# Attention of two entries ahead of the FFN, with the last keys' scores of two head pairs on quarters of the array

## The chip, the cores and the metric

One Trainium2 chip, one core of it. The metric is the device time of one execution in microseconds (us), lower is better. Three runs of the kernel before gave 1162.48, 1165.79 and 1167.2 us; the median is 1165.79.

## The reference

Three blocks follow each other, for 4 batch entries of 448 positions, in fp32 throughout:

```python
# attention: 12 heads of 64, scores capped by tanh
scores = cap * tanh(q @ k.T / sqrt(64) / cap)
attn = softmax(scores)
x = attn @ v                       # heads joined: 4 x 448 x 768
# FFN with LayerNorm and residual, d_ff = 3072
x = x + relu(layernorm(x) * g_ln @ w_ch1) @ w_ch2
# gMLP
h = relu(x @ w_in); u, v = halves of h (512 each)
v_s = w_spatial @ normalize(v) + b_spatial[:, None]
out = (u * v_s) @ w_out
```

## The kernel before

Everything is held transposed: channels on the 128 partitions, the 448 positions along the free axis. Two heads make a pair that fills 128 partitions (64 channels each), so an entry has 6 pairs and the program 24.

**Attention of a pair** (`emit_load`, `emit_s`, `emit_st`, `emit_v`, `emit_n`). The 448 keys are three chunks of 128 and a tail of 64, the "last keys". Scores come out with keys on the partitions. `emit_s` makes the scores of chunks with two fp32 matmuls each (64 x 128 weights, the two heads on the two row halves of the array) into one double PSUM bank ("two"; there are 2); `expo` applies tanh and exp on ScalarE (ACT), the second in place in SBUF ("es"). `emit_st` makes the last keys' scores of both heads in one full-array matmul: the weights hold the last 64 keys of the two heads as diagonal blocks (extra 128 columns of the tile "qk", loaded by two small DMAs, zero elsewhere). `emit_v` adds the exponentials of the chunks on VectorE (DVE), multiplies them with v (128 x 64 weights, the two heads on the two column halves) and with ones (the softmax sums). The last keys' part of v is a full-array matmul with diagonal blocks; the last keys' part of the sums is another one with the constant `blocks` in the first 16 heads, and is folded into the DVE sum (`fold`) in later ones. Sums are inverted by `invert`, by way of DRAM: two rows out, repacked onto 128 partitions, reciprocal, back, broadcast; `FAST` lists the pair that takes the reciprocal directly instead. `emit_n` multiplies, and adds to LayerNorm's sum over channels.

An fp32 matmul shows as two instructions in the trace. "bank" is one of 4 single PSUM banks, "hs" a 128 x 448 SBUF tile, "vt" the tile of v.

**FFN and gMLP** use fp32r with each operand split into a high and a low part, three matmuls per product. Weights come from DRAM in their raw 64-bit form; `weight` rebuilds them (ACT, DVE), keeps a copy in DRAM ("kept") for the next use, and splits them (`wh` slots). `h_unit` is one 128-channel block of the hidden layer for one entry (18 matmuls), `y_unit` one block of the output (12 matmuls); NG = 6 groups of 4 hidden blocks. `ln_mean` and `ln_scale` make LayerNorm; the latter has matmuls of two columns and a round trip by DRAM.

**Order of the work.** `main` writes the program order. Before: the pairs of entry 0 and two pairs of entry 1 (`LEAD = 4` heads) run without FFN beside them (the lead), with 5 weight blocks of w1 prepared early (`EARLY`). Then 2 groups (`SOLO`) of entry 0 run alone, with entry 1's other four pairs between them, then the same 2 groups of entry 1, then the other 4 groups for both entries, which share each weight block. The 12 pairs of entries 2 and 3 are spread between these units. The gMLP of entries 0 and 1 follows, then FFN and gMLP of entries 2 and 3.

`attend` gives each step of a pair its place, in units of one pair's share. `Program` records all operations, gives each a due time from `Recorder`'s cost estimates, and `plan` writes each engine's final order by list scheduling: an engine takes the ready operation that is due first, not more than 28 us ahead (`AHEAD`), if its buffers fit. `prog.either` lets the planner choose between two engines; `prog.group` keeps matmuls together. All DMAs are issued on one queue, SP.

Of the kernel before, what the change touches and what calls it, by code (L numbers as in the profile page):

```python
# [34 lines left out]

SOLO = 2, 0
LEAD = 4
FILL = 0.45

AHEAD_HEADS = 12  # L40

LOAD = 1.05


FAST = (), (11,)

COUNTS = 16, 8, 11, 3, 2, 2, 3, 6, 2, 1

# [7 lines left out]

EARLY = 5

# [362 lines left out]
class Recorder:  # L421
# [3 lines left out]
    def __getattr__(self, method):  # L425
# [5 lines left out]
        def record(*args, **kw):  # L431
# [5 lines left out]
            if self.name == "PE":  # L437
                rows = min(kw["rhs"].ap[0][1], kw["out"].ap[0][1])
                cost = 4 * n / 2400 + 0.004 if kw["rhs"].dtype == F32 else n / 2400 + 0.0133
                if rows <= 64:  # L440
                    cost *= 0.55
            elif self.name == "D":
                cost, latency = 0.5, 4 * out.size() / 360e3
            elif self.name == "A":
                cost = (0.13 if psum_in else 0.16) + n / 1200
                cost += 0.094 if hasattr(kw.get("scale"), "tensor") else 0.0
            elif self.name == "P":
                cost = 1.0 if "pow" in repr(args) + repr(kw) else 0.45 + n / 500
            elif method == "reciprocal":
                cost = 0.15 + n / 160  # L450
            elif method in ("tensor_copy", "tensor_scalar") and not psum_in:
                cost = 0.14 + n / 1920
            else:
                cost = 0.14 + n / 960
# [12 lines left out]
def attn_ffn_gmlp_kernel(  # L467
# [35 lines left out]
    def slots(name, n, shape, dt, pool=const):  # L503
# [4 lines left out]
            ("rs", [128, 2, S], F32R), ("rb", [128, 2, DH], F32R), ("hs", [128, S], F32),  # L508
            ("rc", [128, 2 * S // 128], F32), ("w6", [128, DM, 2], I32), ("wr", [128, DM], F32),
            ("wh", [128, 2, DM], F32R), ("es", [128, 2, S], F32), ("qk", [128, 2 * S + 128], F32),  # L510
            ("small", [128, 80], F32)), COUNTS))

    vts = slots("vt", 2, [128, 4, 128], F32)
# [3 lines left out]
    blocks = const.tile([128, 128], F32, name="blocks")  # L517
    ones32 = const.tile([128, 2], F32, name="ones32")
# [93 lines left out]
    xsp = {}  # L612
    sums = {}

    def emit_load(i):
# [16 lines left out]
        raws[i] = t, u  # L632

# [5 lines left out]
    def emit_s(i, cs):  # L639

        t, u = raws[i]
        scs = [twos.get()[:, :, 0:S] for _ in cs]
# [24 lines left out]
    def invert(name, rows, outs):  # L667

        n = len(rows)
        d0 = dram.tile([n, S], F32, name=f"sum_{name}")  # L670
        d1 = dram.tile([n, S], F32, name=f"inv_{name}")
        c = rcs.get()
# [11 lines left out]

    def emit_v(i):


        b, h = heads[i]
        E = st.pop(i)
        u, et = st.pop(("t", i))  # L690
        s = es.get()
        add(s, E[0], E[1])
        add(s, s, E[2])
        fold = i >= H + LEAD
        if fold:
            for half in range(2):
                r = slice(64 * half, 64 * half + 64)
                add(s[r, half], s[r, half], et[r])
        ps, pr = banks.get()[:, 0:S], banks.get()[:, 0:S]
        with prog.group(0.4):  # L700
            T.matmul(out=ps, lhsT=u[:, 3], rhs=et, start=True, stop=False)
            if not fold:
                T.matmul(out=pr, lhsT=blocks, rhs=et, start=True, stop=False)
            for o, e, w in [(ps, e, u[:, c]) for c, e in enumerate(E)] + [(pr, s, None)]:
                for half in range(2):
                    r = slice(64 * half, 64 * half + 64)
                    T.matmul(out=o[r], lhsT=ones64 if w is None else w[:, r], rhs=e[:, half],
                             start=fold and w is None, stop=e is E[-1] or w is None)
        x, R = xts[b][h // 2] if b < 2 else hs.get(), hs.get()
        cp(x, ps, (A, V))  # L710
        if b < 2 and h + 1 in FAST[b]:
            V.reciprocal(R, pr)
        else:
            cp(R, pr, (A, V))
            invert(f"{b}_{h}", [R[0:1], R[64:65]], [R[0:64], R[64:128]])
        sums[i] = x, R

# [148 lines left out]
    def sp_unit(b, i, sp, bias):  # L866
# [10 lines left out]
        mm3(ps, terms)  # L877
        w, x = hs.get(), hs.get()
        V.tensor_tensor(w, ps, bias, ALU.add)
        with prog.either():  # L880
            for e in (V, P):
                e.tensor_tensor(x, w, us[b][i], ALU.mult)
        if b % 2:
# [85 lines left out]

    def attend(first, n, per, start=0.0, ahead=True):  # L970
        todo = []
        for j in range(0, n, 2):
            i = first + j
            t = start + per * j
# [3 lines left out]
            todo += [(t + x * per, fn, a) for x, fn, *a in stages if ahead or a[0] < first + n]  # L978
        return todo

    def norm(b, t):
        return [(t, ln_mean, (b,))]

    def main():
        emit_load(0)
        SP.dma_start(out=capt, in_=cap)
        SP.dma_start(out=g_t, in_=g_ln)
        P.memset(ones64, 1.0)
        P.memset(blocks, 0.0)
        for half in range(2):  # L990
            r = slice(64 * half, 64 * half + 64)
            P.memset(blocks[r, r], 1.0)
        P.memset(ones32, 1.0)
# [7 lines left out]
        group = FG * 3 * KD + KD * 3 * FG  # L1001
        more = H + LEAD
        for p in range(NP):
            one, two = bs = (2 * p, 2 * p + 1)
            solo = SOLO[p]
            end = H * (two + 1)

            def alone(b):
                return chain(*(x for g in range(solo) for x in (h_units((b,), g, 2), y_units((b,), g, False))))


            n = end - more
            total = solo * group
            per = max(total, 1) * FILL / max(n, 1)
            if p:
                drive(alone(one), attend(more, n, per) + ([(per * (n + 2.3), ln_load, (two,))] + norm(two, per * (n + 2.3) + 1e-6) if n else []))
            else:
                drive(alone(one), attend(more, n, per) + norm(two, per * (n + 2.3)))
            more = end
# [5 lines left out]
            drive(units, attend(more, n, total / max(n, 1), ahead=False))  # L1025
            more += n
            nxt = [] if p + 1 == NP else [two + 1] if AHEAD_HEADS < H else [two + 1, two + 2]
            gmlp(bs, nxt)
            emit_load(more)

    main()
    with tc.manual_schedule():
        t = tok_t[0][0]
        nc.vector.memset(t[:], 0.0)
        nc.scalar.activation(out=t[:], in_=t[:], func=ACTF.Tanh)
        for t in vts.tiles:
            nc.gpsimd.memset(t[:], 0.0)
        for t in qks.tiles:
            nc.gpsimd.memset(t[:, 2 * S:2 * S + 128], 0.0)
        prog.issue()  # L1040
# [54 lines left out]
```

## Time and profile before

| what | value |
|---|---|
| median of three runs | 1165.79 us |
| the profiled execution, device time | 1166.69 us |
| its span, first to last instruction | 1164.9 us |
| TensorE (PE) busy | 1131.2 us, 97% of the span |
| weight loads (PEld) | 916.9 us, 79% |
| VectorE (DVE) | 715.0 us, 61% |
| ScalarE (ACT) | 430.2 us, 37% |
| mean granted TensorE clock | 0.993 |

The profile is one execution, traced by the hardware. Busy time is the union of an engine's instructions. Matmuls are pipelined and their ends are modelled, so the distance from one start to the next tells more than an instruction's own duration, and a TensorE that is always busy need not be at its peak. A wait names what ended it: the engine and the tile that it released. The granted clock is a share of TensorE's full speed.

### The profile page before, as it was taken

To read this page: it belongs to the slowest core of one execution; us is meant where nothing else is said; L and a number is where in the kernel's file an instruction comes from. 1 tells how busy PE (TensorE), PEld (TensorE's weight loads), DVE (VectorE), ACT (ScalarE), POOL (GpSimd) and SP (SyncE) were. 2 spreads that over 40 slices of the span, in tenths; PEclk is the share of its full clock that TensorE was granted. 3 is DMA by queue.
4 is the path that set the end of the run, shared out by engine and by line. 5 is a ranking of instruction groups with operands and counts; after the bars stand their busy time and mean duration, and the time that the engine had idled before them with its cause. 6 is when DMAs were issued, how large, how long until landed. Compare 5 with 4: busy or idle time off the path is not lost.

```text
span 1164.9 us, 14179 instructions
## 1 busy us (share of the span) xinstructions
PE 1131.2 (97%) x5300; PEld 916.9 (79%) x5300; DVE 715.0 (61%) x1188; ACT 430.2 (37%) x638; POOL 22.2 (2%) x30
## 2 busy tenths in 40 slices
PE   7979989999999999999989989999999999999998
PEld 2326667878887777787769779999999999998878
DVE  5548788767576666766979883534343434384751
ACT  6978636344344444344433451011111111120311
POOL 0000000000000000000000100000000000000010
PEclk9999999999999999999999999899999999999999
DMA  7545556556355545655366422212121212124302
GB/s 217 154 116 160 148 158 192 142 172 185 115 165 156 158 134 167 196 158 150 124 187 210 165 70 66 64 52 63 47 69 41 68 41 68 42 71 118 111 17 104
DMA packets 88577, 140.97 MB, mean 121 GB/s; under 512 B 41486, under 2 KB 53692, under 8 KB 88508
## 3 DMA queue, kind: packets, MB, share of 16 engines
q1 hardware_dynamic: 88508, 140.06, 40.7%
q8 instruction: 42, 0.69, 0.2%
q14 instruction: 27, 0.22, 0.1%
HBM read 107.99 MB, written 32.03 MB: 120 GB/s over the span
## 4 chain that ended last, share of the span: by engine, by line
PE 86%; DMA 7%; DVE 4%; SPq 2%; ACT 1%; issue 1%; ACTq 0%; DVEq 0%
PE bank L459 80%; PE two L459 5%; DMA w<-in_w_u_dram 2%; SPq L459 2%; DVE wr L459 1%; DMA hs<-inv 1%; DMA rc<-sum 1%; DMA wr<-kept_w 1%; DVE wh L459 1%; DMA qk<-in_qk_dram 1%; DMA inv<-rc 1%; DVE hs L459 0%; DVE x L459 0%; ACT es L459 0%; DMA w<-in_w_dram 0%
## 5 line engine op out<-in xcount | busy, mean ns | idle before, releaser
L459 PE MATMUL bank<-rs,wh 128*128 128x448 f32 x2070 | 428.5, 366 | 5.1 <-ACT es L459 4.1
L459 PEld LDWEIGHTS bank<-rs,wh 128*128 128x128 f32 x2070 | 389.9, 189 | 41.2 <-ACT es L459 4.6
L459 PE MATMUL bank<-rb,wh 128*128 128x448 f32 x1872 | 391.6, 368 | 7.2 <-ACT wh L459 2.1
L459 PEld LDWEIGHTS bank<-rb,wh 128*128 128x128 f32 x1872 | 353.6, 190 | 43.6 <-issue 5.4
L459 ACT ACTIVATE wh<-wr 128x512 fp32r<-128x512 f32 (+1 forms) x101 | 72.1, 714 | 236.5 <-PE bank L459 201.1
L459 DVE TENSOR_TENSOR x<-bank,x 128x448 f32<-128x448 f32 x144 | 89.6, 623 | 100.9 <-PE bank L459 99.8
L459 ACT ACTIVATE rb<-bank 128x448 fp32r<-128x448 f32 x96 | 52.4, 546 | 239.2 <-PE bank L459 239.2
L459 DVE TENSOR_TENSOR wh<-wr,wh 128x512 fp32r<-128x512 f32 (+1 forms) x167 | 130.2, 781 | 9.5 <-ACT wh L459 4.9
L459 DVE SCALAR_TENSOR_TENSOR rb<-bank,rb 128x448 fp32r<-128x448 f32 x96 | 59.9, 624 | 111.7 <-ACT rb L459 111.4
L459 DVE SCALAR_TENSOR_TENSOR wr<-w,wr 128x512 int32<-128x512 int32 (+1 forms) x152 | 120.4, 792 | 2.5
L459 ACT ACTIVATE wr<-w 128x512 f32<-128x512 f32 (+1 forms) x76 | 57.4, 756 | 81.4 <-DVE wh L459 24.8
L459 ACT ACTIVATE es<-two,qsc 128x896 f32<-128x896 f32 x72 | 70.3, 1004 | 26.6 <-PE two L459 26.6
L459 PE MATMUL two<-qk 64*128 64x448 f32 x288 | 71.8, 591 | 8.5 <-ACT es L459 4.2
L459 ACT ACTIVATE es<-es,capt 128x896 f32<-128x896 f32 x72 | 72.5, 1040 | 0.0
L459 DVE CAST wh<-wr 128x512 fp32r<-128x512 f32 (+1 forms) x66 | 30.7, 466 | 65.7 <-PE bank L459 45.6
L459 DVE TENSOR_TENSOR es<-es,es 128x896 f32<-128x896 f32 x48 | 52.1, 1086 | 23.3 <-ACT es L459 23.0
L459 PE MATMUL bank<-es,vt 128*64 128x448 f32 x288 | 59.4, 548 | 0.0
L459 PEld LDWEIGHTS two<-qk 64*128 64x128 f32 x288 | 25.4, 192 | 40.8 <-issue 21.2
L459 ACT ACTIVATE hs<-bank 128x448 f32<-128x448 f32 x54 | 29.4, 545 | 72.9 <-PE bank L459 69.7
L459 DVE TENSOR_SCALAR wr<-wr 128x512 int32<-128x512 int32 (+1 forms) x76 | 35.8, 472 | 26.4 <-ACT wr L459 26.4
L459 PEld LDWEIGHTS bank<-es,vt 128*64 128x64 f32 x288 | 18.5, 136 | 37.9 <-issue 34.2
L459 PE MATMUL bank<-rs,rb 128*128 128x448 f32 (+1 forms) x192 | 43.7, 381 | 0.0
(86 smaller groups left out, 666.8 us busy)
## 6 DMA issues: line engine op xcount, KB each, us to landing
w<-in_w_dram SPq DMA_DIRECT2D x24, 768.0 KB
w<-in_w_dram SPq DMA_DIRECT2D x36, 512.0 KB
wr<-kept_w SPq DMA_DIRECT2D x32, 384.0 KB
wr<-kept_w SPq DMA_DIRECT2D x48, 256.0 KB
qk<-in_qk_dram SPq DMA_DIRECT2D x48, 224.0 KB
kept_w<-wr SPq DMA_DIRECT2D x24, 384.0 KB
kept_w<-wr SPq DMA_DIRECT2D x36, 256.0 KB
out_dram<-hs SPq DMA_DIRECT2D x24, 224.0 KB
```

Source lines behind the costliest of these rows:

```text
L459: fn(*(put(a) for a in args), **{k: put(a) for k, a in kw.items()})
```

## The change

- `emit_st` serves two pairs at once: for each of four heads one 64 x 64 matmul, on its own quarter of the array. The two pairs of a couple write different halves of the output partitions (`place`), their two heads different banks. The block-diagonal weights in "qk", their DMAs and memsets go.
- `emit_v`: the last keys' v is a fourth step like the chunks, two column halves of 128 x 64, with zeros in the rows of the other pair of the couple (two "vt" tiles, one for each half). The fold into the DVE sum holds for all heads; `blocks` goes. For entries 0 and 1 the products are emitted in two parts, (0, 1) and (2, 3), with scores of the next pair between them. For entries 2 and 3 the sums of a couple are made together, on four 32-column tiles, and inverted together.
- All 24 heads of entries 0 and 1 run ahead of the FFN; the solo units go, and all six groups serve both entries. `EARLY` falls from 5 to 2.
- Loads: q and k of a pair two pairs ahead, early in the step; v by itself, one pair ahead. `invert` sends its rows in one DMA.
- `sp_unit` works in place; "es" has 7 slots instead of 6, "hs" 10 instead of 11. The planner's cost of fp32 matmuls goes by the share of the array.

```diff
-SOLO = 2, 0
-LEAD = 4
-FILL = 0.45
-AHEAD_HEADS = 12
+LOAD_QK = 0.15
 LOAD = 1.05
-FAST = (), (11,)
-COUNTS = 16, 8, 11, 3, 2, 2, 3, 6, 2, 1
+ST = 0.12
+FAST = 22,
+COUNTS = 16, 8, 10, 3, 2, 2, 3, 7, 2, 1
-EARLY = 5
+EARLY = 2
...
     def emit_load(i):
-        t, u = qks.get(), vts.get()
+        t = raws[i] = qks.get()
         for half in range(2):
-            r = slice(64 * half, 64 * half + 64)
-            SP.dma_start(out=t[r, 0:2 * S], in_=qk[b, h + half, r])
-        for half in range(2):
-            r = slice(64 * half, 64 * half + 64)
-            SP.dma_start(out=t[r, 2 * S + 64 * half:2 * S + 64 * half + 64], in_=qk[b, h + half, r, S + TAIL:2 * S])
+            SP.dma_start(out=t[64 * half:64 * half + 64], in_=qk[b, h + half, 64 * half:64 * half + 64])
+    def place(i):
+        return slice(64, 128) if i // 2 % 2 else slice(0, 64)
+    def emit_load_v(i):
+        u = raws["v", i] = vts[i // 2 % 2].get()
+        p = place(i)
...
             SP.dma_start(out=u[:, 0:3, r], in_=v[b, h + half, :, 0:3])
-            SP.dma_start(out=u[r, 3, r], in_=v[b, h + half, r, 3])
+            SP.dma_start(out=u[p, 3, r], in_=v[b, h + half, p, 3])
...
     def emit_st(i):
-        t, u = raws.pop(i)
-        sc = banks.get()[:, 0:S]
-        T.matmul(out=sc, lhsT=t[:, 2 * S:2 * S + 128], rhs=t[:, 0:S], start=True, stop=True)
-        st["t", i] = u, expo(sc, hs.get())
+        scs = [banks.get()[:, 0:S] for _ in range(2)]
+        with prog.group(0.1):
+            for j in (i, i + 2):
+                t = raws[j]
+                for half, sc in enumerate(scs):
+                    r = slice(64 * half, 64 * half + 64)
+                    T.matmul(out=sc[place(j)], lhsT=t[r, S + TAIL:2 * S], rhs=t[r, 0:S], start=True, stop=True)
+        st["t", i] = st["t", i + 2] = [expo(sc, hs.get()) for sc in scs]
...
-        for j, r in enumerate(rows):
-            SP.dma_start(out=d0[j:j + 1], in_=r)
+        SP.dma_start(out=d0, in_=rows)
...
+    def alone(i):
+        return i < 2 * H
+    def products(i, ps, E, ns):
+        u = raws["v", i]
+        for n in ns:
             for half in range(2):
                 r = slice(64 * half, 64 * half + 64)
+                T.matmul(out=ps[r], lhsT=u[:, n, r], rhs=E[n][half], start=n == 0, stop=n == 3)
...
+        now = todo[:] if i // 2 % 2 or alone(i) else []
+        pr = banks.get()[:, 0:S] if now else None
+        width = 64 if len(now) == 1 else 32
+        with prog.group(0.4 if 0 in ns else 0.2):
+            products(i, ps, E, ns)
+            for n, (_, a, _) in enumerate(now):
                 for half in range(2):
+                    q = (2 * n + half) * width
+                    T.matmul(out=pr[q:q + width], lhsT=ones64[:, 0:width], rhs=a[:, half], start=True, stop=True)
...
     def sp_unit(b, i, sp, bias):
-        w, x = hs.get(), hs.get()
-        V.tensor_tensor(w, ps, bias, ALU.add)
+        x = hs.get()
+        V.tensor_tensor(x, ps, bias, ALU.add)
...
     def attend(first, n, per):
-            stages = [(0.0, emit_s, i, (0, 1)), (LOAD, emit_load, i + 2), (0.9, emit_s, i, (2,)),
-                      (0.95, emit_st, i), (2.1, emit_v, i), (4.2, emit_n, i)]
+            stages = [(0.0, emit_s, i, (0, 1)), (0.1, emit_s, i, (2,)), (LOAD_QK, emit_load, i + 4),
+                      (LOAD, emit_load_v, i + 2)]
+            if i < 2 * H:
+                stages += [(2.05, emit_v, i, (0, 1)), (2.15, emit_v, i, (2, 3))]
+            else:
+                stages += [(2.05, emit_v, i)]
+            if i // 2 % 2 == 0:
+                stages += [(ST, emit_st, i)]
...
     def main():
-        lead = attend(0, H, 1.0) + norm(0, H + 2.25) + attend(H, LEAD, 1.0, H)
+        lead = attend(0, 2 * H, 1.0) + [(H + 2.25, ln_mean, (0,)), (2 * H + 2.25, ln_mean, (1,))]
...
-            units = chain(alone(two), *(x for g in range(solo, NG) for x in (
+            units = chain(*(x for g in range(NG) for x in (
                 h_units(bs, g, 3 if g == 0 else 2), y_units(bs, g, g == NG - 1))))
-            total = (2 * NG - solo) * group
-            n = H + AHEAD_HEADS if p + 1 < NP else 0
+            n = 2 * H if p + 1 < NP else 0
```

## Rows read from the trace of the kernel before

**Rows 1.** Busy time by stretch: us, PE, PEld, DVE, ACT, POOL, granted clock, DMA share, GB/s.
```profile
0.00:94.00 94.00, 77.44 (x289) 27.42 (x290) 50.20 (x74) 72.76 (x96) 2.12 (x14) 1.00 0.60 160
94.00:208.00 114.00, 108.06 (x496) 79.06 (x496) 98.28 (x165) 68.34 (x102) 1.42 (x1) 1.00 0.57 165
208.00:575.00 367.00, 367.00 (x1751) 288.67 (x1750) 256.53 (x409) 158.91 (x220) 1.01 (x1) 1.00 0.53 155
```
**Rows 2.** Waits of PE, whole run: who waited for whom, us in total, times, longest.
```profile
PE two L459 <- ACT es L459: 4.2, 4, 1.5
PE two L459 <- DMA qk<-in_qk_dram: 4.2, 1, 4.2
PE bank L459 <- ACT es L459: 4.1, 1, 4.1
PE bank L459 <- DMA qk<-in_qk_dram: 3.9, 2, 2.3
PE bank L459 <- DVE wh L459: 2.3, 4, 1.2
```
**Rows 3.** Timeline of PE, one pair of the lead: start, us, engine, line, instructions.
```profile
43.86 1.77 PE L459 MATMUL two<-qk 64*128 64x448 f32 x8
45.56 1.02 PE L459 MATMUL bank<-hs,vt 128*128 128x448 f32 x2
46.42 0.92 PE L459 MATMUL bank<-hs,blocks 128*128 128x448 f32 x2
47.26 2.48 PE L459 MATMUL bank<-es,vt 128*64 128x448 f32 x12
49.57 0.92 PE L459 MATMUL bank<-es,ones 128*64 128x448 f32 x4
50.42 1.02 PE L459 MATMUL two<-qk 64*128 64x448 f32 x4
51.37 1.02 PE L459 MATMUL bank<-qk 128*128 128x448 f32 x2
52.32 1.77 PE L459 MATMUL two<-qk 64*128 64x448 f32 x8
```
**Rows 4.** Timeline of PE, a later pair's products among FFN units.
```profile
415.60 1.02 PE L459 MATMUL bank<-hs,vt 128*128 128x448 f32 x2
416.55 2.48 PE L459 MATMUL bank<-es,vt 128*64 128x448 f32 x12
418.85 0.92 PE L459 MATMUL bank<-es,ones 128*64 128x448 f32 x4
419.70 2.67 PE L459 MATMUL bank<-rb,wh 128*128 128x448 f32 x12
```
**Rows 5.** Groups of DVE by shape, whole run: count, busy us, mean ns, idle before.
```profile
L459 DVE TENSOR_TENSOR es<-es,hs 64x448 f32<-64x448 f32 x32 | 19.7, 617 | 0.9
```
**Rows 6.** Timeline of the SP queue in the lead: three DMA issues.
```profile
61.47 1.76 SPq L459 DMA_DIRECT2D vt<-in_v_dram  x3
```
**Rows 7.** Timeline of ACT in the same pair of the lead.
```profile
43.97 0.64 ACT L459 ACTIVATE hs<-bank,qsc 128x448 f32<-128x448 f32 x1
44.50 1.03 ACT L459 ACTIVATE es<-es,capt 128x896 f32<-128x896 f32 x1
45.43 0.66 ACT L459 ACTIVATE hs<-hs,capt 128x448 f32<-128x448 f32 x1
45.99 1.89 ACT L459 ACTIVATE es<-two,qsc 128x896 f32<-128x896 f32 x2
47.77 1.97 ACT L459 ACTIVATE es<-es,capt 128x896 f32<-128x896 f32 x2
49.81 0.55 ACT L459 ACTIVATE x<-bank 128x448 f32<-128x448 f32 x1
```
**Rows 8.** Timeline of PE at ln_scale of entries 2 and 3.
```profile
728.60 3.27 PE L459 MATMUL bank<-ones,hs 128*112 128x2 f32 x16
```
**Rows 9.** Busy time of the 20 us around it; columns as in rows 1.
```profile
720.00:740.00 20.00, 20.00 (x86) 18.44 (x85) 4.75 (x12) 1.63 (x3) 2.02 (x2) 0.83 0.22 48
```

More of the change, by code (lines that the diff above doesn't have):

```diff
@@ L437, in record @@
             if self.name == "PE":
[L438 to L441, printed above, removed]
+                cost = n / 2400 + 0.0133
+                if kw["rhs"].dtype == F32:
+                    part = kw["rhs"].ap[0][1] * kw["out"].ap[0][1] / 128 ** 2
+                    cost = (4 * n / 2400 + 0.004) * part + (0.004 if part < 1 else 0.0)
             elif self.name == "D":
@@ L508, in attn_ffn_gmlp_kernel @@
             ("rs", [128, 2, S], F32R), ("rb", [128, 2, DH], F32R), ("hs", [128, S], F32),
-            ("rc", [128, 2 * S // 128], F32), ("w6", [128, DM, 2], I32), ("wr", [128, DM], F32),
-            ("wh", [128, 2, DM], F32R), ("es", [128, 2, S], F32), ("qk", [128, 2 * S + 128], F32),
+            ("rc", [128, 4 * S // 128], F32), ("w6", [128, DM, 2], I32), ("wr", [128, DM], F32),
+            ("wh", [128, 2, DM], F32R), ("es", [128, 2, S], F32), ("qk", [128, 2 * S], F32),
             ("small", [128, 80], F32)), COUNTS))
-    vts = slots("vt", 2, [128, 4, 128], F32)
+    vts = [slots(f"vt{i}_", 1, [128, 4, 128], F32) for i in range(2)]
     xts = [[const.tile([128, S], F32, name=f"x{i}_{k}") for k in range(KD)] for i in range(2)]
@@ L516, in attn_ffn_gmlp_kernel @@
     ones64 = const.tile([128, 64], F32, name="ones64")
-    blocks = const.tile([128, 128], F32, name="blocks")
     ones32 = const.tile([128, 2], F32, name="ones32")
@@ L613, in attn_ffn_gmlp_kernel @@
     sums = {}
+    todo = []
     def emit_load(i):
@@ L620, in emit_load @@
         b, h = heads[i]
-        t, u = qks.get(), vts.get()
+        t = raws[i] = qks.get()
         for half in range(2):
-            r = slice(64 * half, 64 * half + 64)
-            SP.dma_start(out=t[r, 0:2 * S], in_=qk[b, h + half, r])
-        for half in range(2):
-            r = slice(64 * half, 64 * half + 64)
-            SP.dma_start(out=t[r, 2 * S + 64 * half:2 * S + 64 * half + 64], in_=qk[b, h + half, r, S + TAIL:2 * S])
+            SP.dma_start(out=t[64 * half:64 * half + 64], in_=qk[b, h + half, 64 * half:64 * half + 64])
+    def place(i):
+        return slice(64, 128) if i // 2 % 2 else slice(0, 64)
+    def emit_load_v(i):
+        if i >= len(heads):
+            return
+        b, h = heads[i]
+        u = raws["v", i] = vts[i // 2 % 2].get()
+        p = place(i)
         for half in range(2):
@@ L639, in emit_s @@
     def emit_s(i, cs):
-        t, u = raws[i]
+        t = raws[i]
         scs = [twos.get()[:, :, 0:S] for _ in cs]
@@ L667, in invert @@
     def invert(name, rows, outs):
-        n = len(rows)
+        n = len(outs)
         d0 = dram.tile([n, S], F32, name=f"sum_{name}")
         d1 = dram.tile([n, S], F32, name=f"inv_{name}")
-        c = rcs.get()
+        c = rcs.get()[:, 0:n * S // 128]
         def packed(d):
             return d.rearrange("a n -> (a n)").rearrange("(p m) -> p m", p=128)
-        for j, r in enumerate(rows):
-            SP.dma_start(out=d0[j:j + 1], in_=r)
+        SP.dma_start(out=d0, in_=rows)
         SP.dma_start(out=c, in_=packed(d0))
@@ L683, in invert @@
             SP.dma_start(out=o, in_=d1[j:j + 1].partition_broadcast(64))
[L685 to L695, printed above, removed]
+    def alone(i):
[3 more added lines that the diff above has]
+        for n in ns:
             for half in range(2):
                 r = slice(64 * half, 64 * half + 64)
[L698 to L704, printed above, removed]
-                for half in range(2):
[L706 to L712, printed above, removed]
-        else:
-            cp(R, pr, (A, V))
-            invert(f"{b}_{h}", [R[0:1], R[64:65]], [R[0:64], R[64:128]])
-        sums[i] = x, R
@@ new lines, in products, with emit_v @@
+                T.matmul(out=ps[r], lhsT=u[:, n, r], rhs=E[n][half], start=n == 0, stop=n == 3)
+    def emit_v(i, ns=range(4)):
+        b, h = heads[i]
+        if 0 in ns:
+            E = st[i]
+            s = es.get()
+            add(s, E[0], E[1])
+            add(s, s, E[2])
+            et = st.pop(("t", i))
+            p = place(i)
+            for half in range(2):
+                add(s[p, half], s[p, half], et[half][p])
+            st[i] = s, banks.get()[:, 0:S], [[e[:, half] for half in range(2)] for e in E] + [et]
+        s, ps, E = st[i]
+        if 3 not in ns:
+            with prog.group(0.2):
+                products(i, ps, E, ns)
+            return
+        x = xts[b][h // 2] if b < 2 else hs.get()
+        todo.append((i, s, x))
+        now = todo[:] if i // 2 % 2 or alone(i) else []
+        pr = banks.get()[:, 0:S] if now else None
+        width = 64 if len(now) == 1 else 32
+        with prog.group(0.4 if 0 in ns else 0.2):
+            products(i, ps, E, ns)
+            for n, (_, a, _) in enumerate(now):
+                for half in range(2):
+                    q = (2 * n + half) * width
+                    T.matmul(out=pr[q:q + width], lhsT=ones64[:, 0:width], rhs=a[:, half], start=True, stop=True)
+        del st[i], raws["v", i]
+        cp(x, ps, (V, A))
+        if not now:
+            return
+        todo.clear()
+        R = [hs.get() for _ in now]
+        if i in FAST:
+            V.reciprocal(R[0], pr)
+        else:
+            cp(R[0], pr, (V, A))
+            invert(f"{b}_{h}", R[0][0:128:width], [r[half:half + 64] for r in R for half in (0, 64)])
+        for (j, _, y), r in zip(now, R):
+            sums[j] = y, r
@@ L968, in drive, with attend @@
             fn(*args)
-    def attend(first, n, per, start=0.0, ahead=True):
+    def attend(first, n, per):
         todo = []
@@ L973, in attend @@
             i = first + j
-            t = start + per * j
-            stages = [(0.0, emit_s, i, (0, 1)), (LOAD, emit_load, i + 2), (0.9, emit_s, i, (2,)),
-                      (0.95, emit_st, i), (2.1, emit_v, i), (4.2, emit_n, i)]
-            todo += [(t + x * per, fn, a) for x, fn, *a in stages if ahead or a[0] < first + n]
-        return todo
-    def norm(b, t):
-        return [(t, ln_mean, (b,))]
+            t = per * j
+            stages = [(0.0, emit_s, i, (0, 1)), (0.1, emit_s, i, (2,)), (LOAD_QK, emit_load, i + 4),
[6 more added lines that the diff above has]
+                stages += [(ST, emit_st, i)]
+            if alone(i):
+                stages += [(4.2, emit_n, i)]
+            elif i // 2 % 2:
+                stages += [(4.2, emit_n, i - 2), (4.2, emit_n, i)]
+            todo += [(t + x * per, fn, a) for x, fn, *a in stages]
+        return todo
     def main():
         emit_load(0)
+        emit_load(2)
+        emit_load_v(0)
         SP.dma_start(out=capt, in_=cap)
@@ L988, in main @@
         P.memset(ones64, 1.0)
[L989 to L992, printed above, removed]
         P.memset(ones32, 1.0)
@@ L996, in main @@
         V.tensor_scalar(out=qsc, in0=qsc, scalar1=float(D) ** -0.5, scalar2=None, op0=ALU.mult)
-        lead = attend(0, H, 1.0) + norm(0, H + 2.25) + attend(H, LEAD, 1.0, H)
+        lead = attend(0, 2 * H, 1.0) + [(H + 2.25, ln_mean, (0,)), (2 * H + 2.25, ln_mean, (1,))]
         lead += [(1.0 + j * H / EARLY, make, ("w1", j)) for j in range(EARLY)]
         drive([], lead)
-        group = FG * 3 * KD + KD * 3 * FG
-        more = H + LEAD
         for p in range(NP):
[L1004 to L1019, printed above, removed]
-            units = chain(alone(two), *(x for g in range(solo, NG) for x in (
-                h_units(bs, g, 3 if g == 0 else 2), y_units(bs, g, g == NG - 1))))
-            total = (2 * NG - solo) * group
-            n = H + AHEAD_HEADS if p + 1 < NP else 0
[L1025 to L1029, printed above, removed]
+            bs = 2 * p, 2 * p + 1
+            units = chain(*(x for g in range(NG) for x in (
+                h_units(bs, g, 3 if g == 0 else 2), y_units(bs, g, g == NG - 1))))
+            n = 2 * H if p + 1 < NP else 0
+            drive(units, attend(2 * H * (p + 1), n, 2 * NG * (FG * 3 * KD + KD * 3 * FG) / max(n, 1)))
+            gmlp(bs, [b for b in (2 * p + 2, 2 * p + 3) if n])
     main()
@@ L1035, in attn_ffn_gmlp_kernel @@
         nc.scalar.activation(out=t[:], in_=t[:], func=ACTF.Tanh)
[L1036 to L1039, printed above, removed]
+        for p, u in zip((slice(64, 128), slice(0, 64)), vts):
+            nc.gpsimd.memset(u.tiles[0][p, 3], 0.0)
         prog.issue()
```

3 lines of the change are left out of this document (1 added, 2 removed).

## The prediction

> **What bounds the kernel now.** I read the stages first: three stretches up to the first gMLP, each with the busy time of every engine [rows 1]. TensorE is busy 77.4 of 94 us while the first eight head pairs run alone (the lead), 108.1 of 114 us while four more pairs run among the "solo" FFN units and all 367 us in the long stretch where twelve pairs run among the FFN units of two entries. So TensorE's work sets the time, and the lead is the one stage with much to win by waiting less. There ACT (72.8) is nearly as busy as TensorE, DVE is not (50.2). TensorE's waits say how little there is elsewhere [rows 2]: 4.2 us for score banks that ACT has not emptied, 4.2 and 3.9 us for the loads of q and k (at the start, and for the small copies of the last keys), 4.1 us once in the gMLP, 2.3 us for weights in the solo stretch. An edit is therefore priced by the TensorE time that it takes or gives, then by what it does to these waits.
>
> **Sum against what.** Rows come from one execution of 1166.69 us (span 1164.9, 1.8 us around it), 0.9 us over the median of three. These three lie within 0.4% of each other; 0.5%, some 6 us, is about what a measurement here can tell from no change.
>
> **The change, part by part.** The price of each form is the distance between starts in one undisturbed pair of the lead [rows 3]: scores of two chunks 1.70 us, last keys' values (hs,vt) 0.86, their sums (blocks) 0.84, values of three chunks (es,vt, 12 instructions) 2.31, sums (ones) 0.85, third chunk's scores 0.95, last keys' scores (qk) 0.95; together 8.46 us. In later pairs the blocks step is folded into the sums already, and the forms cost 0.95 (hs,vt), 2.30 and 0.85 [rows 4], so with 1.70, 0.95 and 0.95 from the lead a pair is 7.7 us.
>
> Last keys' scores: one full-array product per pair becomes four products on quarters for two pairs. No quarter stands in the trace. The nearest rows bound it: if quarters run side by side, 0.95 us for two pairs (two halves by rows and two by columns do run side by side: 2.31 us for 12 column instructions is 0.77 per two products, and 1.70 us for four row-half products is 0.85 per two); if they queue, four times some 0.77, 3.1 us. I take 0.95, since both directions overlap in rows, so 0.48 per pair.
>
> Last keys' values: block-diagonal full-array product becomes a fourth column pair inside the same run, 0.77 instead of 0.86 to 0.95, and the mode change disappears. Blocks: 0.84 us in eight pairs go; two 64-row DVE adds of 0.617 us take their place [rows 5], in a lead where DVE has 44 us free [rows 1].
>
> Sums of entries 2 and 3: two pairs share one run on four 32-wide columns. Not in the trace either: 0.85 us for both if they overlap like the 64-wide ones, 3.1 us if they queue. I take 0.85 plus 0.1 for the mode change, about what a switch adds in rows 3 (0.95 for an isolated step, 0.85 inside a run). The Trainium skill, "TensorE: Matmul & The Clock Gate", Part 3: Packing small matmuls, says that a weight load overlaps running matmuls only when it goes to another row group. By that rule the loads of column tiles, which share the row group, would be exposed, and this step would grow by eight loads, an estimate of some 1 us per two pairs and 6 us in all. The rows do not bear it out: three chunks of two column tiles run in 2.31 us, three times 0.77, with no room for exposed loads between them [rows 3].
>
> Products in two parts, with scores between, in the first 24 heads: values of two chunks about 1.6 us (8 instructions, between 0.85 for 4 and 2.31 for 12), then two more chunks and the sums 2.31. The number of mode changes per pair hardly changes: before, scores, full array, columns, scores, full array, scores; after, scores, columns, scores, (quarters,) columns, scores. Taken as nothing; at worst two more at 0.1 to 0.2 us, 12 pairs, 2 to 5 us.
>
> So a pair of the first two entries costs 1.70 + 1.6 + 0.95 + 0.48 + 2.31 = 7.04 us and one of the others 1.70 + 0.95 + 0.48 + 2.30 + 0.77 + 0.48 = 6.7. Eight pairs of the lead give 8 x 1.42 = 11.4, four solo pairs 4 x 0.7 = 2.7, twelve pairs 12 x 1.0 = 12.2: **TensorE has 26.3 us less to do.** In a stretch that is 367 of 367 busy the last 12 us count in full.
>
> The solo units go: 8 blocks of w1 and 12 of w2 are no longer prepared a second time. TensorE multiplies as much as before; DVE, ACT and DMA save. I take nothing but the 2.3 us of waits for weights [rows 2], and those I use up below. Loads: per pair eight DMAs become six, and the sums leave in one DMA of several rows instead of two; at 0.59 us an issue [rows 6] SP gets over 1 us per pair back. Of the move, q and k of the pair after next are issued ahead of everything else of a pair; the last keys' scores of a couple need the second pair's load, which is why it is issued second at the start. The wait for the small copies of the keys, most of 3.9 us [rows 2], goes; early weights fall from five to two, so that more weights must be made after the lead.
>
> What is late next: the lead has 12 pairs instead of 8. ACT's pitch, start to start, is 0.53 and 0.56 for the last keys' two steps, 0.93 for a chunk's exp and 0.89 for its tanh [rows 7]: 3 x 1.82 + 1.09 = 6.55 us per pair, under TensorE's 7.04, but LayerNorm of entry 0, two weights and some copies from PSUM come on top, so that both stand near 8 us. FFN units of entry 0 that are ready may fill TensorE's gaps late in the lead. Then LayerNorm of entry 1, which before ran beside four pairs and solo units, has only entry 0's first units (four h units) over it. Before, the lead and the solo stretch left TensorE 16.6 + 5.9 = 22.5 us idle [rows 1]. I put 24.5 for the same work after: 4 less (key copies, weights), 6 more in the lead and at the hand-over. That is +2.
>
> The two ln_scale groups now come one behind the other. At the other pair of entries they do so already: sixteen 2-column matmuls, 3.3 us, and the granted clock of that 20 us slice is 0.83, with TensorE showing no idle time [rows 8, 9]; at 0.17 of 20 us that is 3.4 us of work between the two levels of 1.2 and 2.4 GHz. At even odds, +1.5.
>
> The gMLP gets a seventh es slot and one hs slot less, its product in place: nothing, as its adds and multiplies stay; its one 4.1 us wait may go or come back elsewhere.
>
> Sum: 1166.7 - 26.3 + 2 + 1.5 = **1144 us.**
>
> **The rivals.** (a) *The lead and the hand-over starve.* ACT takes the copies, two of 0.55 us a pair [rows 7], so 6.55 + 1.1 = 7.65, and with its part of LayerNorm and weights I estimate 8 us a pair instead of 7.04, 12 x 0.96 = 11.5 us, or TensorE waits as long for entry 1's LayerNorm: 1144 + 12 = 1156. For it: ACT 72.8 of 94 already with eight pairs [rows 1], 4.2 us of waits on it [rows 2]. Against: units of entry 0 as filling. The Trainium skill, "TensorEngine Tiling (Array Packing)", PSUM Bottleneck, says the same: tiling speeds up TensorE, not the emptying of PSUM, which may become the limit. (b) *The new tiles do not overlap.* Quarters queue (12 x 2.1 = 26 us) and the 32-wide columns too (6 x 2.2 = 13): 1144 + 39 = 1183, slower than before. It decides from 23 us on, that is once the 18 groups cost 1.3 us more than I take. Against it: both kinds of halves overlap [rows 3]. One direction alone overlapping gives 1.5 us a group, +10 or 1154. (c) *Better covered.* The solo stretch's 5.9 us [rows 1] and the gMLP's 4.1 us [rows 2] with the clock it costs go, too: 1144 - 13 = 1131. (d) *It does not do what it says:* the written-out order of the planner takes back in waits what the array gives, as the hand-over loses (a) twice: 1168.
>
> **How the numbers follow.** Forecast 0.50, (a) 0.22, (b) 0.06, (c) 0.14, (d) 0.08. The forecast, (a) and (c) lie below 1160 but for an upper edge of 0.03, and a third of (b), with one direction overlapping, does too: faster 0.85. Half of (d) and that edge: within 0.5% 0.07. The rest of (b) and half of (d): slower 0.08. The range goes from (c) to just above (a), 1130 to 1158; beyond it lie (b), (d) and the edges, 0.2.
>
> **What would show it.** Quarters: eight instructions in about 0.95 us, over 1.5 refutes the step. 32-wide sums: eight in 0.85 to 0.95. A pair of the lead near 7.0 us where nothing waits; over 7.8 with waits on ACT means (a). The stretch of twelve pairs: every pair 1.0 us shorter. First units of entry 1: an idle stretch of TensorE over 5 us there, ended by DVE, means (a) at the hand-over. The forecast is wrong if TensorE's idle time up to the end of the second group's units is not between 18 and 31 us, or its busy time does not fall by some 25.

## The result and the profile after

The changed kernel takes 1119.8 us (median of 4, 1116.59 to 1120.62) against 1164.13 for the kernel before beside it; the ratio is 0.9614, interval 0.958 to 0.9648. I forecast 1144 and a range of 1130 to 1158: the direction was right, the gain of 44 us is twice what I gave it. The profiled execution after is the fastest of its four, so the two traces differ by 50.1 us of span, some 6 more than the medians.

Stage lengths, from the starts of the first matmul of each stage in the two TensorE timelines; idle is the sum of TensorE's waits in the stage:

| stage | before, us (idle) | after, us (idle) | difference |
|---|---|---|---|
| attention and FFN up to the first gMLP | 575.0 (22.3) | 542.2 (11.1) | -32.8 |
| first gMLP, to ln_scale of entries 2, 3 | 153.6 (7.5) | 140.1 (0.4) | -13.5 |
| FFN of entries 2, 3 | 322.9 (0) | 320.2 (0) | -2.7 |
| second gMLP and end | 113.4 | 112.2 | -1.2 |

Where TensorE works at a low clock, no idle time shows it. Low clock is counted here as its busy time in slices of 1 us, times the share of the clock that is missing in the slice. Up to the first gMLP it costs nothing before and 2.8 us after, in the first gMLP 4.7 us before and nothing after, in the FFN of entries 2 and 3 3.4 us before and nothing after.

TensorE's waits after, the answer to [rows 2] (who waited for whom: us, times, longest):

```profile
PE two L455 <- DMA qk<-in_qk_dram: 4.3, 1, 4.3
PE bank L455 <- DVE acc L455: 4.1, 1, 4.1
PE bank L455 <- ACT x L455: 0.9, 1, 0.9
PE bank L455 <- DMA vt<-in_v_dram: 0.9, 1, 0.9
PE bank L455 <- ACT hs L455: 0.6, 1, 0.6
PE bank L455 <- DVE rb L455: 0.4, 1, 0.4
PE bank L455 <- DVE hs L455: 0.4, 1, 0.4
```

The waits for score banks, for the small copies of the keys, for weights and for the gMLP's evictions are gone. The wait for LayerNorm's sum is not new: [rows 2] leaves out the line of the kernel before on it, its fifth largest:

```profile
PE bank L459 <- DVE acc L459: 3.8, 2, 2.7
```

A pair of the lead, TensorE's timeline, beside [rows 3]:

```profile
34.23 1.77 PE L455 MATMUL two<-qk 64*128 64x448 f32 x8
35.93 1.72 PE L455 MATMUL bank<-es,vt 128*64 128x448 f32 x8
37.59 1.02 PE L455 MATMUL two<-qk 64*128 64x448 f32 x4
38.54 0.98 PE L455 MATMUL bank<-qk 64*64 64x448 f32 x8
39.45 0.97 PE L455 MATMUL bank<-es,vt 128*64 128x448 f32 x4
40.25 0.92 PE L455 MATMUL bank<-hs,vt 128*64 128x448 f32 x4
41.00 0.92 PE L455 MATMUL bank<-es,ones 128*64 128x448 f32 x4
41.85 1.77 PE L455 MATMUL two<-qk 64*128 64x448 f32 x8
```

The quarters (64*64) take 0.91 us for two pairs, so they do run side by side. This pair takes 7.62 us; the next, without quarters, 6.72. The mean of 7.17 stands beside my 7.04, for pairs that nothing disturbs. Of the twelve groups of quarters nine take 0.91 to 0.98 us; the three others, in the lead, take 1.71 to 2.05. In one of these a weight load of the quarters waits for the second pair's q and k, and TensorE's list of waits does not show it:

```profile
53.69 0.19 PEld L455 LDWEIGHTS bank<-qk 64*64 64x64 f32 x2 [0.61 <-DMA qk<-in_qk_dram]
```

A pair of entries 2 and 3 in the same view, beside [rows 4]:

```profile
257.68 2.48 PE L455 MATMUL bank<-es,vt 128*64 128x448 f32 x12
259.98 0.92 PE L455 MATMUL bank<-hs,vt 128*64 128x448 f32 x4
260.83 0.96 PE L455 MATMUL bank<-es,ones 128*32 128x448 f32 x8
261.72 1.02 PE L455 MATMUL two<-qk 64*128 64x448 f32 x4
```

The four 32-wide columns take 0.89 us for two pairs. The estimate in my prediction by the rule of the Trainium skill, "TensorE: Matmul & The Clock Gate", Part 3: Packing small matmuls, would have made it some 1 us more; here, too, the measurement speaks against exposed loads.

### The profile page after: what moved, and what is told of

It reads as the page before. It is cut to its first block, busy times and chain, and to the rows that moved or that the text cites. A ratio compares the mean times of both kernels' runs of the same rounds, so it can differ in the third digit from the quotient of the medians.

```text
span 1114.8 us, 14169 instructions
## 1 busy us (share of the span) xinstructions
PE 1099.8 (99%) x5380; PEld 900.5 (81%) x5380; DVE 704.9 (63%) x1178; ACT 414.9 (37%) x614; POOL 19.7 (2%) x23
## 4 chain that ended last, share of the span: by engine, by line
PE 94%; DMA 3%; DVE 1%; SPq 1%; issue 0%; ACT 0%; DVEq 0%
PE bank L455 87%; PE two L455 7%; DMA hs<-inv 1%; SPq L455 1%; DMA qk<-in_qk_dram 1%; DMA rc<-sum 1%; DMA sum<-hs 0%; DMA vt<-in_v_dram 0%; DVE hs L455 0%; DVE es L455 0%; DVE wr L455 0%; DVE x L455 0%; DMA inv<-rc 0%; ACT hs L455 0%; DVE rb L455 0%
## 5 line engine op out<-in xcount | busy, mean ns | idle before, releaser
L455 PE MATMUL bank<-rs,wh 128*128 128x448 f32 x2088 | 423.8, 362 | 0.0
L455 PE MATMUL bank<-rb,wh 128*128 128x448 f32 x1872 | 379.5, 362 | 0.4 <-DVE rb L455 0.4
L455 ACT ACTIVATE wh<-wr 128x512 fp32r<-128x512 f32 (+1 forms) x91 | 64.8, 713 | 209.1 <-PE bank L455 164.6
L455 DVE TENSOR_TENSOR wh<-wr,wh 128x512 fp32r<-128x512 f32 (+1 forms) x150 | 117.3, 782 | 11.3 <-ACT wh L455 6.8
L455 PE MATMUL two<-qk 64*128 64x448 f32 x288 | 69.5, 584 | 4.3 <-DMA qk<-in_qk_dram 4.3
L455 DVE CAST wh<-wr 128x512 fp32r<-128x512 f32 (+1 forms) x59 | 27.7, 469 | 61.8 <-PE bank L455 44.5
L455 PE MATMUL bank<-es,vt 128*64 128x448 f32 x288 | 63.7, 557 | 0.9 <-DMA vt<-in_v_dram 0.9
L455 ACT ACTIVATE hs<-bank 128x448 f32<-128x448 f32 x50 | 27.1, 542 | 76.5 <-PE bank L455 76.5
```

Of the source, the lines that this page charges most:

```text
L455: fn(*(put(a) for a in args), **{k: put(a) for k, a in kw.items()})
```

## The experiments

The kernel before ran beside each series, with medians of 1163.9 to 1165.4 us; the times below are medians. The series ran on different chips, so between series the ratio to the kernel before is the safer number.

**The order alone** (kernel before: twelve pairs ahead, no solo units).

```diff
-SOLO = 2, 0
-LEAD = 4
+SOLO = 0, 0
+LEAD = 12
-EARLY = 5
+EARLY = 2
-        fold = i >= H + LEAD
+        fold = i >= 16
```

> The kernel before, with only the order of the change: twelve pairs ahead of the FFN, no solo units, two early weight blocks; tiles, sums and loads as before. Theory A (the extra gain over my sum is the order's: without solo units TensorE waits 11 us less up to the first gMLP, and the gMLP's gap is a matter of its own): 1153 us, idle up to the gMLP near 11 us, the gap of 4 us in the gMLP still there. Theory B (the order takes waits away only together with the shorter tiles, which leave TensorE's pairs below ACT's): 1160 to 1168, idle near 22 us. If the gMLP's gap goes with the order as well: 1145.

Measured 1157.1, ratio 0.9937 (0.9907 to 0.9968). In the traces the gain comes from the gMLP, which takes 142.2 us instead of 153.6, and 2.2 us from the FFN after it; the stretch up to the gMLP takes 578.4, longer than before, and is idle for 22.3 us as before. It is longer by low clock, 6.4 us behind waits of 4.5, 2.7 and 2.5 us; without that it would be 3 us shorter than before. Its waits, same view as above:

```profile
PE bank L459 <- DMA qk<-in_qk_dram: 9.9, 4, 4.5
PE two L459 <- DMA qk<-in_qk_dram: 4.1, 1, 4.1
PE bank L459 <- DVE acc L459: 2.7, 1, 2.7
```

So leaving out the solo units bought no idle time up to the gMLP; there theory B holds. That the gap of the gMLP went as well was the branch that I had put at 1145; the measured time fits neither that nor theory B's 1160 to 1168.

**The order and the split** (in addition, the products of the first 24 heads in two halves; `emit_v` takes the chunks of a half as an argument, and the last keys' product comes last instead of first).

```diff
             stages = [(0.0, emit_s, i, (0, 1)), (LOAD, emit_load, i + 2), (0.9, emit_s, i, (2,)),
                       (0.95, emit_st, i), (2.1, emit_v, i), (4.2, emit_n, i)]
+            if i < 2 * H:
+                stages = [(0.0, emit_s, i, (0, 1)), (0.1, emit_s, i, (2,)), (0.12, emit_st, i), (LOAD, emit_load, i + 2),
+                          (2.05, emit_v, i, (0, 1)), (2.15, emit_v, i, (2, 3)), (4.2, emit_n, i)]
```

> The order alone as in the first series, and its products of the first 24 heads in two halves with the third chunk's scores and the last keys' scores between them; tiles and loads still as before. Theory E (the places of the scores take the waits away, whatever the tiles): idle up to the first gMLP from 22 to some 13 us, 1147 us. Rival M (they pay only once TensorE's share of a pair is shorter than ACT's chain, which needs the new tiles): 1154 to 1158, idle above 18 us.

Measured 1149.1, ratio 0.986 (0.9808 to 0.9911). Idle time up to the gMLP falls to 15.2 us with the tiles of before, and 6.4 of that is one wait for LayerNorm's sum:

```profile
PE bank L459 <- DVE acc L459: 6.4, 1, 6.4
PE two L459 <- DMA qk<-in_qk_dram: 4.2, 1, 4.2
PE bank L459 <- DVE wh L459: 3.3, 1, 3.3
PE bank L459 <- DMA qk<-in_qk_dram: 1.1, 1, 1.1
```

The loads stand where they stood in the program, and yet the waits for the small copies fall from 9.9 to 1.1. I take it that with the scores of a pair made earlier, its tile of q and k comes free earlier; no run tests that by itself. Undisturbed pairs take 8.77 us instead of 8.46, so with the old tiles the split does cost TensorE time, 0.3 us a pair, and gains all the same. Theory E.

**The split alone** (kernel before, solo units and eight pairs ahead; the same edit of `attend` and `emit_v`).

> The kernel before, with the products of the first 24 heads in two halves and the scores between, and nothing else: solo units, eight pairs in the lead. Theory E: idle up to the first gMLP from 22 to some 15 us, 1158 us. Rival M: 1162 to 1167, no difference that can be told. The gap of the gMLP may go or stay in both.

Measured 1167.8, ratio 1.0039 (0.9999 to 1.0079). Idle time falls by 5 us to 17.1, but the stretch up to the gMLP grows from 575.0 to 580.9: TensorE is granted 0.91 on average between 140 and 200 us, which costs 4.9 us of work, in three stretches that each follow a wait (2.7 us on q and k, 1.8 and 2.0 us on weights), and a pair of the lead takes 8.77 us instead of 8.46, as in the run before. The gap of the gMLP stays (2.9 us). For this kernel rival M holds.

**The change without the split** (changed kernel; products in one piece).

```diff
-            if i < 2 * H:
+            if i < 0:
                 stages += [(2.05, emit_v, i, (0, 1)), (2.15, emit_v, i, (2, 3))]
```

> The changed kernel with the products of the first 24 heads in one piece instead of two halves with scores between. Theory E (the scores between the halves keep ACT fed and TensorE from waiting): idle up to the first gMLP goes from 11 to some 18 us, 1127 us. Rival F (the halves only cost mode changes): 1117 us, idle as it was.

Measured 1137.8, ratio 0.977 (0.9744 to 0.9796): **18 us slower than the changed kernel.** Idle up to the gMLP is 25.8 us, 14.7 more, and low clock costs 3.8 us more; together they are 18.5 of the 19.5 us by which that stretch is longer. Its first waits, and a stretch of its lead in TensorE's timeline:

```profile
PE two L455 <- ACT es L455: 9.6, 6, 3.0
PE two L455 <- DMA qk<-in_qk_dram: 4.2, 1, 4.2
PE bank L455 <- DVE acc L455: 4.1, 1, 4.1
```

```profile
27.90 2.48 PE L455 MATMUL bank<-es,vt 128*64 128x448 f32 x12
30.20 0.92 PE L455 MATMUL bank<-hs,vt 128*64 128x448 f32 x4
30.95 0.92 PE L455 MATMUL bank<-es,ones 128*64 128x448 f32 x4
31.80 1.77 PE L455 MATMUL two<-qk 64*128 64x448 f32 x8
35.02 1.02 PE L455 MATMUL two<-qk 64*128 64x448 f32 x4 [1.44 <-ACT es L455]
```

The products run in one stretch of 3.9 us (27.90 to 31.80), scores follow in a bunch, and TensorE then waits for a score bank that ACT has not emptied. In the changed kernel there is no such wait at all: the next score bank is filled between the halves while ACT works on the one before.

**The last keys on the full array again** (changed kernel; block-diagonal scores and values per pair).

```diff
-        scs = [banks.get()[:, 0:S] for _ in range(2)]
...
+        sc = banks.get()[:, 0:S]
+        T.matmul(out=sc, lhsT=t[:, 2 * S:2 * S + 128], rhs=t[:, 0:S], start=True, stop=True)
...
+            if n == 3:
+                T.matmul(out=ps, lhsT=u[:, 3], rhs=E[3], start=False, stop=True)
```

> The changed kernel with the last keys back on the full array: block-diagonal scores per pair and block-diagonal v, everything else as changed. Theory A (TensorE's work counts in full in all 24 pairs): 24 x 0.47 for the scores and 24 x 0.1 to 0.2 for the values, +14, 1134 us. Theory B (the lead is ACT's, so that only the twelve later pairs count): +7, 1127 us. The two extra small loads of a pair may add up to 3 us of wait at the start in both.

Measured 1131.7, ratio 0.9716 (0.969 to 0.9742), 11.9 us slower. The stretch up to the gMLP is 12.3 us longer with 1 us less idle and the same low clock, so TensorE has 13.3 us more to do. Theory A: what the quarters save counts in full, in the lead, too.

**The same with late loads.**

```diff
-            stages = [(0.0, emit_s, i, (0, 1)), (0.1, emit_s, i, (2,)), (LOAD_QK, emit_load, i + 4),
+            stages = [(0.0, emit_s, i, (0, 1)), (0.1, emit_s, i, (2,)), (LOAD, emit_load, i + 2),
...
-        emit_load(2)
```

> The kernel with the last keys on the full array, with q and k loaded one pair ahead at the place of the kernel before instead of two pairs ahead. Theory L (the early loads are what took the waits out of the lead): waits on the loads of q and k come back as with the order alone (9.9 us there), 1138 to 1141 us against 1131.7. Rival (the loads are hidden anyway): 1132 us.

Measured 1133.4, ratio 0.9734 (0.9708 to 0.976), idle 12.3 us against 10.1. Theory L falls: the waits on q and k are 8.8 us against 7.8, and the 1.7 us between the medians are no difference that can be told.

**Sums apart** (changed kernel).

```diff
     def alone(i):
-        return i < 2 * H
+        return True
```

> The changed kernel with each pair's sums on its own two 64-wide columns and its own inversion in entries 2 and 3, as in entries 0 and 1; nothing else. Theory A (only TensorE's work counts): six runs of 0.85 more, less a mode change each, +4 to 5, 1124.5 us. Theory C (the smaller number of small DMAs on SP is what closed the gap of the gMLP): that gap of 4 us and the lower clock after it come back, +11, 1131 us.

Measured 1128.2, ratio 0.9682 (0.9654 to 0.971), 8.4 us slower, between the two. Up to the gMLP 9.4 us are added, 3.8 of them idle time and 1.9 low clock; the other 3.7 are the work that theory A counts. The gap of the gMLP does not come back, so theory C falls.

**The order with the fold everywhere** (kernel before; the first edit, and `fold = True`).

> The order alone as in the first series, and the last keys' sums folded into the DVE sum for all heads, so that the blocks product is gone. Theory A (TensorE's work counts in full also in the lead): eight products of 0.84 us, -6.8 against 1157.1, 1150 us. Rival (the two more adds a pair make TensorE wait for DVE's sum in the lead): 1154 to 1157, with more waits on es ended by DVE than the 2.7 us of the order alone.

Measured 1165.6, ratio 1.0011 (0.9979 to 1.0043): 8 us slower than the order alone. Its ten runs spread from 1159.3 to 1173.1, and the profiled one, the fastest, is only 2.9 us slower than the profiled one of the order alone, so the traces account for some 3 of the 8 us. TensorE's work up to the gMLP fell as computed (581.2 - 31.5 = 549.7 us, against 578.4 - 22.3 = 556.1), but its idle time rose to 31.5 us, and not by the adds:

```profile
PE bank L459 <- DMA qk<-in_qk_dram: 16.7, 9, 4.5
PE two L459 <- ACT es L459: 8.6, 7, 1.5
```

Shorter pairs with the scores at their old places meet the loads and ACT sooner, as I read these waits. Both theories had the reason wrong.

**The gap of the gMLP.** In the kernel before, the SP queue at the first gMLP (start, time, DMAs), then ACT and TensorE:

```profile
590.05 0.58 SPq L459 DMA_DIRECT2D sum<-hs  x2
594.72 0.34 SPq L459 DMA_DIRECT2D rc<-sum  x1
595.17 0.37 SPq L459 DMA_DIRECT2D w<-in_w_u_dram  x1
...
600.08 0.33 SPq L459 DMA_DIRECT2D w<-in_w_u_dram  x1
```

```profile
607.39 0.89 ACT L459 ACTIVATE wr<-w 128x768 f32<-128x768 f32 x1 [5.40 <-DMA w<-in_w_u_dram]
608.17 1.07 ACT L459 ACTIVATE es<-bank 128x512 f32<-128x512 f32 x2
```

```profile
608.81 31.94 PE L459 MATMUL bank<-rs,wh 128*128 128x448 f32 x144 [4.13 <-ACT es L459]
```

The read-back of a late pair's sums (rc) waits some 4 us for them to land, with the third w_u block behind it; ACT can start on the fourth at 607.4; and on ACT the evictions of the gMLP's first products stand behind that block's first step. Two edits of the kernel before try this. First, the read-backs of three pairs are held back by the planner:

```diff
+LATE = 30.0
...
+        for i, more in self.late.items():
+            due[i] += more
...
+        if name in ("3_4", "3_6", "3_8"):
+            prog.late[len(prog.ops)] = LATE
         SP.dma_start(out=c, in_=packed(d0))
```

> The kernel before, unchanged but for one thing: the planner holds back the read-back of the sums of three of the last pairs, so that on SP it no longer stands ahead of the loads of the last w_u blocks at the start of the first gMLP. Theory S (the gap of 4.1 us there is SP's head of line: the read-back waits for its own sums to land, the weight behind it comes late, and the evictions of the gMLP's first products stand behind that weight's first step on ACT): the gap and the low clock after it go, 4.1 and some 4 us, 1156 to 1157 us. Rival (DVE is late there whatever SP does): 1164, gap of 3 to 4 us as before.

Measured 1177.1, ratio 1.0118 (1.0077 to 1.0159); the profiled execution is the slowest of six. The gap shrinks to 1.2 us, but the tiles that wait for their sums are missing later: waits of 5.3 and 4.2 us on hs follow, with low clocks after them. A muddled test. Second, one of these pairs is inverted directly on DVE:

```diff
-        if b < 2 and h + 1 in FAST[b]:
+        if (b < 2 and h + 1 in FAST[b]) or (b, h) == (3, 4):
```

> The kernel before, with the sums of one late pair (entry 3, heads 4 and 5) inverted directly on DVE as the last pair of entry 1 is, so that its round trip by DRAM does not stand ahead of the third block of w_u on SP. Theory S (SP's head of line makes the gap of the gMLP): the gap goes from 4.1 to about 1 us or less and the low clock after it goes, 1155 to 1158 us. Rival (DVE is what is late; it gets 2.8 us more): gap as before or longer, 1165 to 1168.

Measured 1156.8, ratio 0.9929 (0.9899 to 0.996): 7 us, from an edit that concerns one pair.

```profile
597.67 0.32 SPq L459 DMA_DIRECT2D kept_wu<-wr  x1
598.09 0.38 SPq L459 DMA_DIRECT2D w<-in_w_u_dram  x1
...
603.27 0.38 SPq L459 DMA_DIRECT2D w<-in_w_u_dram  x1
```

```profile
609.53 30.02 PE L459 MATMUL bank<-rs,wh 128*128 128x448 f32 x144 [0.85 <-ACT es L459]
```

The gap is 0.85 us, and the slice from 600 to 620 us runs at 1.00 instead of 0.83. Counted from the gMLP's first matmul (579.0 here, 575.0 before), the last w_u block is issued 0.8 us earlier, and ACT can start on it 4.8 us after the issue (608.10) instead of 7.3. So of the 3.3 us by which ACT has that block sooner only 0.8 come from the place on SP and 2.5 from the time between issue and start. The round trip of that pair's sums is the cause of the gap; how much of it by its place on SP, by its traffic or by what else the planner moved with it was not told apart. With the order alone and in the changed kernel the last w_u block is issued 19.9 and 20.3 us after the gMLP's first matmul instead of 25.1, and ACT does not wait for it; in the changed kernel:

```profile
562.55 0.37 SPq L455 DMA_DIRECT2D w<-in_w_u_dram  x1
```

```profile
568.91 0.91 ACT L455 ACTIVATE wr<-w 128x768 f32<-128x768 f32 x1 [1.03 <-DVE wh L455]
```

The stages of the kernel with that one pair inverted directly change by +4.0, -8.2 and -2.7 us up to the gMLP, in it and in the FFN after it, so the 7 us are not the gap alone.

**LayerNorm's mean later, and the last pair of entry 0 inverted directly** (changed kernel, one edit each).

```diff
-        lead = attend(0, 2 * H, 1.0) + [(H + 2.25, ln_mean, (0,)), (2 * H + 2.25, ln_mean, (1,))]
+        lead = attend(0, 2 * H, 1.0) + [(H + 4.25, ln_mean, (0,)), (2 * H + 2.25, ln_mean, (1,))]
```

> The changed kernel with LayerNorm's mean of entry 0 emitted one pair later in the lead (H + 4.25 instead of H + 2.25), so that its matmul does not wait for the inverted sums. Theory D (the 4.1 us wait for acc costs itself and the low clock of 0.83 in the 20 us after it): both go, 1112 us. Rival: LayerNorm comes too late for the hand-over and TensorE waits there as long: 1118 to 1121.

Measured 1117.1, ratio 0.9591 (0.9568 to 0.9615): at best half of the 7 us. The wait for acc is still 3.1 us, but the lead keeps its full clock; waits of 3.7 us on ACT come instead.

```diff
-FAST = 22,
+FAST = 10, 22
```

> The changed kernel with the last pair of entry 0 inverted directly on DVE (FAST = 10, 22), so that LayerNorm's mean does not wait for the round trip of its sums. Theory D (that wait of 4.1 us and the low clock after it): both go, 1112 to 1114 us. Rival (DVE's 2.95 us delay the sums of the pairs beside it as much): 1118 to 1121.

Measured **1114.0, ratio 0.9559 (0.9515 to 0.9602).** That is 5.8 us below the changed kernel; all six runs are below its four, but on another chip, and the intervals of the two ratios just overlap. Idle up to the gMLP is 8.2 us with no low clock, and of the wait for acc 0.2 us are left. The longest waits:

```profile
PE two L455 <- DMA qk<-in_qk_dram: 4.2, 1, 4.2
PE bank L455 <- DVE es L455: 1.3, 1, 1.3
PE bank L455 <- DMA vt<-in_v_dram: 1.2, 1, 1.2
PE two L455 <- ACT es L455: 0.8, 2, 0.4
```

## Why the prediction was wrong

The trace after ends 27.4 us below my sum: 10.0 of these up to the first gMLP, 13.5 in the gMLP, 2.7 and 1.2 behind it. Two of my steps failed, each by some 13 us, and smaller errors the other way hid a part of the first.

**TensorE's work: right.** I computed 26.3 us. Time less idle up to the first gMLP fell from 552.7 to 531.1, 21.6 us. The changed kernel has one stretch of low clock in it, which begins in the wait for LayerNorm's sum (columns as in [rows 1]):

```profile
70.00:73.30 3.30, 0.63 (x8) 0.00 (x0) 1.24 (x4) 2.30 (x3) 0.00 (x0) 1.00 0.50 120
73.30:74.70 1.40, 0.01 (x1) 0.04 (x1) 1.21 (x2) 0.00 (x0) 0.00 (x0) 0.53 0.05 3
74.70:80.10 5.40, 5.40 (x12) 1.70 (x14) 3.82 (x7) 3.54 (x7) 0.00 (x0) 0.50 0.44 104
80.10:85.00 4.90, 4.90 (x24) 1.48 (x20) 4.03 (x7) 3.73 (x7) 0.00 (x0) 0.99 0.26 74
```

TensorE works for 5.4 us at the lower of the clock's two levels (0.50, 1.2 GHz), which costs 2.7 to 2.8 us and makes 24.3. The three late groups of quarters lose some 3 us, 2 of them in no list of waits, about what is still missing; the kernel before may hide such time, too. The prices of the new forms held: quarters 0.91 (taken 0.95), 32-wide sums 0.89 (0.95), two chunks of values 1.66 (1.6). Rival (b) is refuted.

**"Products in two parts ... Taken as nothing": the step that failed.** I looked for its cost in mode changes and missed that it moves the scores. In the changed kernel its cost is indeed about nothing: up to the gMLP, time less idle and low clock is 529.4 us without it and 528.3 with it. But it decides whether the lead waits: 25.8 us idle without it, 11.1 with it, and with the low clock behind the waits 18 us of time. My own test, idle time between 18 and 31 us, is failed. My 24.5 us is nearly what the changed kernel has without the split; the waits on ACT that I feared as rival (a) are there, 9.6 us, and the split is what takes them away. The Trainium skill, "TensorEngine Tiling (Array Packing)", PSUM Bottleneck, says that tiling speeds up TensorE and not the emptying of PSUM, which may become the bottleneck; the kernel without the split agrees, with these 9.6 us.

**"The gMLP ...: nothing": failed, too.** The stage became 13.5 us shorter: 7.1 of waits, the 4.1 us gap and two of 1.9 and 1.5 us near 675 us, and 4.7 of low clock right behind both. I saw the 4.1 us wait in [rows 2], had a part of its price in rival (c), and did not follow it back past "ACT" to the block of weights and the queue. The order alone closes it, with that block issued 5 us sooner; the solo stretch's waits, the other half of (c), it gave back elsewhere in the lead.

**The hand-over and the second clock term.** No wait over 5 us there, and the two ln_scale groups of entries 0 and 1 ran 31 us apart at full clock; my +1.5 was wrong in place, the 2.8 us above stand in its stead, after the wait for acc. For that wait I had no term: its line is the one that [rows 2] leaves out. That the FFN of entries 2 and 3 gained 2.7 us cannot be put down to the change: the clock after the sixteen 2-column matmuls [rows 8, 9] is low in 8 of the 14 traces of this case and not in the other 6. The changed kernel is among the 6, its faster version (FAST = 10, 22) among the 8.

In sum, by medians: the order gives some 7 us, the split with the old tiles 8 more, and the tiles with the rest of the change 29. These depend on each other: the split alone gives nothing, the fold without the split loses 8 us (3 in the traces), and without the split the changed kernel loses 18. Left open: why waits of some 2 us are followed by low clock with the split alone, while the kernel before has one of 2.1 us at 175 us without it, and how the 29 us divide between fewer small DMAs, earlier loads and tiles beyond the 12 and 8 us that were undone singly.

## What to carry to other kernels

An edit that moves work is to be priced by what now stands between two instructions that feed another engine, and not by its mode changes alone: here, score banks refilled between two halves of the products were worth 18 us. Making the bound engine's pieces shorter may gain nothing while the engine that feeds it, and the loads, are served as late as before: the fold without the split was such a case. Follow a wait back through the queues to the first late transfer: the round trip of one pair's 3.5 KB of sums made a gMLP stage wait, and that pair inverted on another path gave back 7 us.

## What was not expected of the hardware

Four 64 x 64 fp32 products on quarters took 0.91 us and four of 128 x 32 0.89 us, about as long as a single full-array product (0.95 at an isolated place [rows 3]). A wait of 4.1 us in the lead was followed by low clock that cost 2.8 us in the changed kernel, and one of 3.1 us in the version with the later mean by none.
